# First rows by whole-unit transfers on one queue, and both weight matrices in a four-row interleaved layout, in a fused linear-attention and MLP kernel

## The chip, the cores and the metric

The kernel runs on one core of one Trainium2 chip. The metric is device time in microseconds (us) for one execution, lower is better. Engines are named as in the profile: PE is TensorE (PEld its weight loads, which overlap the matmuls: before, 130.1 us of loads beside 172.8 us of matmuls in a span of 180.5), DVE is VectorE, ACT is ScalarE, POOL is GpSimd and SP is SyncE. A name such as L507 is a line of that kernel's file, so the numbers differ between kernels.

In the lines of the profile, a is alpha and la its logarithm, cum the running sums of la, b and binv their exponentials, qp and kp the scaled q and k, qkT their transposes, at and atm the scores before and after the mask, yps and x the attention's output, xT its transpose, hT the output of layer 1 and acc that of layer 2. An idle matmul works on zeros and is there to keep PE's clock up (46 of them held the granted clock at 1.00 through a wait in which it otherwise fell to 0.50). W_in's 384 rows are three k-tiles of 128.

## The reference

A gated linear attention feeds a two-layer MLP with tanh-GELU. Inputs and output are float32.

```python
# q, k, v, alpha: (4, 8, 768, 48)
for t in range(S):
    state = alpha[:, :, t, :, None] * state + np.einsum('bhd,bhe->bhde', k[:, :, t], v[:, :, t])
    y[:, :, t] = np.einsum('bhd,bhde->bhe', q[:, :, t], state)
x = y.transpose(0, 2, 1, 3).reshape(3072, 384)
h = x @ w_in                                  # w_in  (384, 2048)
g = 0.5 * h * (1.0 + np.tanh(c * (h + 0.044715 * h * h * h)))
out = g @ w_out                               # w_out (2048, 384)
```

## The kernel before

The sequence is cut into chunks of 128 tokens. A chunk of two batch elements is a pair, one batch element of it is a unit; there are 12 pairs. Pairs 0 and 1 are the first chunk, and their attention is the only work that layer 1 (hT = W_in^T x) has to wait for at the start. A scheduler of the kernel's own fixes the order on each engine; the tile framework then adds a semaphore wait wherever an instruction reads what another, or a transfer, wrote.

Rows of pairs 0 and 1 come packed, a transfer for each four heads of a unit, 32 partitions each, on the queues of SP and ACT. W_in and W_out come on GpSimd's queue, in four parts each, and are narrowed to bf16 on the way (a part is 768 KB of float32 in DRAM and 384 KB as it lands).

```python
LOADS = ('gatea0', 'v0', 'gatek0', 'in 0', 'pk1', 'in 1', 'in 2', 'v1', 'in 3', 'out 0', 'out 1', '2a', ...)
RINGS = (('a', 0, 0, 'SP'), ('a', 0, 2, 'ACT'), ('a', 0, 1, 'SP'), ('a', 0, 3, 'ACT'), ...)   # 20 pieces

self.w_in = const.tile([C, self.NKT, self.d_ff], BF16, name="w_in")      # 128 x 3 x 2048
self.w_out = const.tile([C, self.NFT, self.d_model], BF16, name="w_out")  # 128 x 16 x 384

def load_packed(self, n, c, i, j):            # one of four pieces of a pair
    ...
    src = self.src[n][2 * i + j // 2, j % 2 * 4:j % 2 * 4 + 4, c * C:(c + 1) * C]
    {"SP": nc.sync, "ACT": nc.scalar}.get(e, nc.gpsimd).dma_start(
        u[n][32 * j:32 * j + 32].rearrange("g i (o r) d -> g (i o) (r d)", o=2),
        src.rearrange("y (g r) d -> g y (r d)", r=R))

def wait(self, r, m, j):                      # a "gate": GpSimd's queue stops here
    return lambda e: self.nc.gpsimd.tensor_copy(self.gate[:, 0:1], u[r][:, 0, 0, 0:1])

def load_w(self, which, part):
    if which == "in":
        sl = slice(part * w, (part + 1) * w)                              # w = 512 columns
        self.nc.gpsimd.dma_start(
            self.w_in[:, :, sl], self.w_in_dram.rearrange("(j c) n -> c j n", c=self.C)[:, :, sl])
    else:
        self.nc.gpsimd.dma_start(
            self.w_out[:, sl, :], self.w_out_dram.rearrange("(n c) p -> c n p", c=self.C)[:, sl, :])

def layer1(self, f, c, lo, hi, nt):           # one group: six matmuls
    for s in range(2):
        for j in range(self.NKT):
            self.nc.tensor.matmul(h[:, s], self.w_in[:, j, (nt + s) * self.C:(nt + s + 1) * self.C],
                                  self.xT[c][:, j, lo:hi].rearrange("p g t -> p (g t)"), ...)
```

## Time and profile before

| | before |
|---|---|
| median of 3 runs | 181.46 us (180.95 to 181.86) |
| span of the profiled run | 180.5 us, granted PE clock 1.00 |
| PE busy | 172.8 us, 96% of the span |
| first layer-1 matmul | 17.03 us |
| layer 1 of pairs 0 and 1 ends | 33.05 us |
| from there to the end | 147.45 us |

PE is the bound, so a change is read on PE's lane: when does its first real work start, where does it wait, and how long is the part after the start. In the chain of waits, each line is start, duration, and what the end of the kernel hung on then. In the timeline, the bracket tells how long the engine was idle and what ended it.

### The profile page before, as it was taken

Reading aid. Unit: us, or ns where it says so; the run is one execution under the profiler, and the core shown is the slowest. Engines: PE = TensorE matmul, PEld = TensorE weight load, DVE = VectorE, ACT = ScalarE, POOL = GpSimd, SP = SyncE. Lnnn points to the kernel's source line nnn. Section 1 sums busy time; section 2 is a strip of 40 time slices with the busy share of each in tenths; the row PEclk is TensorE's granted clock in tenths of the full one; section 3 lists DMA queues with packets and bytes.
Section 4 is the critical chain, followed back from the end, with each engine's and each line's share of the span. In section 5 each row is a group of like instructions: output and inputs, shape, how many; then the busy total and the mean of one; then the engine's idle time right before and its main releaser. Section 6 shows DMA issues by size and latency. Waiting matters only on the chain.

```text
span 180.5 us, 4489 instructions
## 1 busy us (share of the span) xinstructions
PE 172.8 (96%) x1858; PEld 130.1 (72%) x1861; DVE 96.9 (54%) x201; ACT 129.8 (72%) x214; POOL 61.1 (34%) x68
## 2 busy tenths in 40 slices
PE   7769999999999999999999999999999999999993
PEld 2446769666796787688688779679677687686872
DVE  7476853045769696487499798199255425000000
ACT  3648768974898678848788757887987984491831
POOL 2595847996657766431740500000000000000000
PEclk9999999999999999999999999999999999999999
DMA  5999999999999999999994535543361280311102
GB/s 154 195 246 210 185 236 229 218 217 205 196 317 212 188 265 227 193 243 229 126 235 128 142 99 131 87 120 79 68 155 52 44 205 4 87 44 47 44 0 87
DMA packets 51204, 27.75 MB, mean 154 GB/s; under 512 B 38832, under 2 KB 48240, under 8 KB 51184
## 3 DMA queue, kind: packets, MB, share of 16 engines
q0 software_dynamic: 32096, 17.70, 63.6%
q1 hardware_dynamic: 18512, 9.38, 19.8%
q10 hardware_dynamic: 576, 0.39, 0.7%
q8 instruction: 14, 0.23, 0.6%
q14 instruction: 6, 0.05, 0.1%
HBM read 25.17 MB, written 4.72 MB: 166 GB/s over the span
## 4 chain that ended last, share of the span: by engine, by line
PE 87%; DMA 8%; POOL 2%; ACT 1%; SPq 1%; issue 0%; POOLq 0%
PE hT L508 35%; PE acc L527 34%; DMA w_in<-in_moe_w_in_dram 5%; PE at L426 4%; PE qkT_ps L365 3%; PE yps L483 3%; PE kv L443 2%; PE cum L321 2%; PE yps L480 2%; DMA k<-in_k_dram 2%; DMA a<-in_alpha_dram 1%; PE xT_ps L497 1%; POOL k L248 1%; PE cum L323 1%; SPq L248 1%; PE idle L223 1%
## 5 line engine op out<-in xcount | busy, mean ns | idle before, releaser
L508 PE MATMUL hT<-xT,w_in 128*128 128x256 bf16 x576 | 69.5, 273 | 0.2 <-DMA w_in<-in_moe_w_in_dram 0.2
L527 PE MATMUL acc<-w_out,gT 128*128 128x384 bf16 (+1 forms) x400 | 69.1, 319 | 0.0
L514 ACT ACTIVATE gT<-hT 128x512 bf16<-128x512 f32 x96 | 56.7, 597 | 16.6 <-PE hT L508 13.3
L508 PEld LDWEIGHTS <-w_in 128*128 128x128 bf16 x576 | 54.3, 98 | 7.3 <-DMA w_in<-in_moe_w_in_dram 0.4
L527 PEld LDWEIGHTS <-gT 128*128 128x128 bf16 x400 | 36.6, 97 | 19.3
L433 DVE TENSOR_TENSOR atm<-at,ut 128x512 bf16<-128x512 f32 x48 | 30.0, 683 | 13.5 <-PE at L426 13.5
L355 DVE TENSOR_TENSOR qp<-q,b 128x768 bf16<-128x768 f32 (+1 forms) x15 | 11.9, 796 | 24.6 <-ACT b L344 23.4
L236 POOL DMA_DIRECT2D v<-in_v_dram x13 | 14.6, 1126 | 13.0 <-PE xT_ps L497 7.8
L539 ACT COPY ot<-acc 128x384 f32<-128x384 f32 (+1 forms) x18 | 8.3, 460 | 13.8 <-PE acc L527 12.9
L236 POOL DMA_DIRECT2D q<-in_q_dram x11 | 12.3, 1117 | 12.3 <-DVE xT L501 7.1
L236 POOL DMA_DIRECT2D a<-in_alpha_dram x11 | 12.3, 1118 | 5.2 <-ACT la L304 1.9
L214 ACT ACT_TABLE_LOAD x9 | 11.5, 1283 | 2.8 <-issue 2.6
L344 ACT ACTIVATE b<-cum 128x768 bf16<-128x768 f32 (+1 forms) x15 | 10.3, 684 | 4.5 <-PE cum L323 2.5
L236 POOL DMA_DIRECT2D k<-in_k_dram x11 | 12.3, 1115 | 2.8 <-DMA w_out<-in_moe_w_out_dram 1.1
L355 DVE TENSOR_TENSOR kp<-k,binv 128x768 bf16<-128x768 f32 (+1 forms) x15 | 11.8, 791 | 0.4 <-DMA k<-in_k_dram 0.4
L514 ACT ACT_TABLE_LOAD x9 | 11.5, 1283 | 0.2
L490 ACT CAST x<-yps 128x384 bf16<-128x384 f32 x15 | 7.2, 479 | 5.3 <-PE yps L483 5.2
L344 ACT ACTIVATE binv<-cum 128x768 bf16<-128x768 f32 (+1 forms) x15 | 10.2, 683 | 0.0
L383 DVE COPY qkT<-qkT_ps 128x1024 bf16<-128x1024 bf16 (+1 forms) x12 | 7.9, 687 | 3.9 <-PE qkT_ps L365 3.8
L223 PE MATMUL idle<-zero 128*128 128x512 bf16 x24 | 8.6, 450 | 1.3 <-DVE half L798 1.2
L465 DVE TENSOR_TENSOR stmp<-kv,st 128x384 f32<-128x384 f32 x16 | 8.8, 551 | 1.2 <-PE kv L443 1.2
L468 DVE TENSOR_TENSOR st<-stmp,ends 128x384 bf16<-128x384 f32 x16 | 8.9, 558 | 0.6
(64 smaller groups left out, 161.0 us busy)
## 6 DMA issues: line engine op xcount, KB each, us to landing
out_dram<-ot SPq DMA_DIRECT2D x23, 192.0 KB, 2.3
a<-in_alpha_dram POOLq DMA_DIRECT2D x9, 384.0 KB, 10.9
q<-in_q_dram POOLq DMA_DIRECT2D x9, 384.0 KB, 10.6
k<-in_k_dram POOLq DMA_DIRECT2D x9, 384.0 KB, 11.2
v<-in_v_dram POOLq DMA_DIRECT2D x11, 192.0 KB, 11.2
w_in<-in_moe_w_in_dram POOLq DMA_DIRECT2D x4, 384.0 KB, 8.4
w_out<-in_moe_w_out_dram POOLq DMA_DIRECT2D x4, 384.0 KB, 9.8
a<-in_alpha_dram SPq DMA_DIRECT2D x6, 96.0 KB, 3.7
```

The source lines that it names most:

```text
L214: nc.scalar.add_instruction(mybir.InstLoadActFuncSet(name=nc.get_next_instruction_name(), act_func_set_id=i, engine=mybir.EngineType.Activ ...
L223: self.nc.tensor.matmul(ps, self.zero[:, 0:self.C], self.zero, start=True, stop=True)
L236: (nc.sync if e == "SP" else nc.gpsimd).dma_start(u[n][:, lo:hi].rearrange("t b h d -> t (b h) d"), src)
L344: self.nc.scalar.activation(u[n].rearrange("t i h d -> t i (h d)")[:, lo:hi], cum, AF.Exp, scale=1.0 if n == "b" else -1.0)
L355: self.nc.vector.tensor_tensor(out, rows, b, op=ALU.mult)
L433: self.nc.vector.tensor_tensor(u["atm", i][:, o], u["at", i][o], self.ut[:, None, :].to_broadcast([self.C, self.H // 2, self.C]), op=ALU.mult)
L465: nc.vector.tensor_tensor(s, acc, old, op=ALU.add)
L468: nc.vector.tensor_tensor(new.rearrange("f p (o d) -> f (p o) d", o=2), acc.rearrange("f p (o d) -> f (p o) d", o=2), ends, op=ALU.mult)
L508: self.nc.tensor.matmul(h[:, s], self.w_in[:, j, (nt + s) * self.C:(nt + s + 1) * self.C], self.xT[c][:, j, lo:hi].rearrange("p g t -> p ( ...
L514: return lambda e: self.nc.scalar.activation(self.gT[c % self.NG][:, nt:nt + 2, lo * self.C:hi * self.C], f.pop(("h", c, lo, nt)), AF.Gelu ...
L527: self.nc.tensor.matmul(f["acc", c, b][:, lo:hi], self.gT[c % self.NG][:, nt, b * self.C:(b + 1) * self.C], self.w_out[:, nt, lo:hi], star ...
L539: self.copy(e)(f["ot", c, b][:, sl], f["acc", c, b] if half is None else f["acc", c, b, half][:, sl])
```

## The change

The intent is to start earlier. A unit's rows become one transfer over all 128 partitions on SP's queue, so the first unit can be worked on while the second is in flight; v of pair 0 comes there too, as float32, and is narrowed by an engine; GpSimd is freed for W_in. For this a partition holds four tokens of two heads in another order, and masks and sums are built for it. W_out is put with four neighbouring rows in a partition (source runs of 6 KB instead of 1.5 KB), and since W_out's row order is the order of layer 1's columns, layer 1 must read W_in's columns in steps of four.

```diff
-    LOADS = ('gatea0', 'v0', 'gatek0', 'in 0', 'pk1', 'in 1', 'in 2', 'v1', 'in 3', 'out 0', ...)
-    RINGS = (('a', 0, 0, 'SP'), ('a', 0, 2, 'ACT'), ('a', 0, 1, 'SP'), ('a', 0, 3, 'ACT'), ...)
+    LOADS = ('gatev0', 'in 0', 'in 1', 'v1', 'in 2', 'in 3', 'out 0', ...)
+    RINGS = (('a', 0, 0, 1), ('a', 0, 1, 2), ('q', 0, 0, 1), ('k', 0, 0, 1), ('q', 0, 1, 2), ('k', 0, 1, 2), ('v', 0, 0, 2),
+             ('a', 1, 0, 1), ('a', 1, 1, 2), ('q', 1, 0, 1), ('k', 1, 0, 1), ('q', 1, 1, 2), ('k', 1, 1, 2))
+    NARROW = (0,)
 ...
+            if u["packed"] and n != "v":
+                dma(u[n][:, lo].rearrange("p (o r) d -> p o (r d)", o=2),
+                    src[0, :, c * C:(c + 1) * C].rearrange("h (g r) d -> g h (r d)", r=R))
 ...
-                    self.w_out[:, sl, :], self.w_out_dram.rearrange("(n c) p -> c n p", c=self.C)[:, sl, :])
+                    self.w_out[:, part * w:(part + 1) * w, :], self.w_out_dram.rearrange("(n c r) p -> n c r p", c=self.C, r=w)[part])
 ...
     def layer1(self, f, c, lo, hi, nt):
+            w_in = self.w_in.rearrange("k j (q c r) -> k j q r c", c=self.C, r=self.NFT // 4)
-                    self.nc.tensor.matmul(h[:, s], self.w_in[:, j, (nt + s) * self.C:(nt + s + 1) * self.C],
+                    self.nc.tensor.matmul(h[:, s], w_in[:, j, nt // 4, nt % 4 + s],
 ... (masks, transposes, scheduler costs, and v narrowed on an engine: cut)
```

More of the change, by code (lines that the diff above doesn't have):

```diff
@@ L17 @@
     cum=530, cum_packed=1500, t8=450, t4=225, attn=340, kv=170, inter=170, intra=205, tx=168, l1_4=655, l1_2=340, l2=655,
-    qk2=910, qk1=500, ev8=650, ev4=350, mask=640, st=1090, st0=545, end=110, attn2=590, xc=520, xe=330, ot=540,
+    qk2=910, qk1=500, ev8=650, ev4=350, mask=640, st=1090, st0=545, end=110, attn2=590, vb=320, vb_act=480, ring=1150, ring_v=1900, ring_issue=450, xc=520, xe=330, ot=540,
     ev8_act=960, ev4_act=520, xc_act=450, xe_act=450, ot_act=450,
-    strip=2120, cast=1500, weight=2080, dma=2100, issue=1100, wissue=760, sp=100, store=2600, turn=1250, landed=2200, xbar_qk=1500, xbar_x=1000, late_x=2500, piece=330, late_k=1500, piece_issue=450, begin=2700, cast_0=1300, share=1200, cast_1=1900, ln_packed=1040, cold=380, fill=216, zero=1100,
+    strip=2120, cast=1500, weight=2080, dma=2100, issue=1100, wissue=760, sp=100, store=2600, turn=1250, landed=2200, xbar_qk=1500, xbar_x=1000, late_x=2500, piece=330, late_k=1500, piece_issue=450, begin=3100, cast_0=1300, share=1200, cast_1=1900, ln_packed=1040, cold=380, fill=216, zero=1100,
 )
@@ L143 @@
     EARLY = (0, 1)
-    LOADS = ('gatea0', 'v0', 'gatek0', 'in 0', 'pk1', 'in 1', 'in 2', 'v1', 'in 3', 'out 0', 'out 1', '2a', 'out 2', '2b', 'out 3', '3', '4', '5', '6', '7', '8', '9', '10', '11')
-    PACKED, CUM_FF, R = (0, 1), (1,), 4
-    RINGS = (('a', 0, 0, 'SP'), ('a', 0, 2, 'ACT'), ('a', 0, 1, 'SP'), ('a', 0, 3, 'ACT'), ('q', 0, 0, 'SP'), ('q', 0, 2, 'ACT'), ('q', 0, 1, 'SP'), ('q', 0, 3, 'ACT'), ('k', 0, 0, 'SP'), ('k', 0, 2, 'SP'), ('k', 0, 1, 'SP'), ('k', 0, 3, 'SP'), ('a', 1, 0, 'SP'), ('a', 1, 1, 'SP'), ('a', 1, 2, 'SP'), ('a', 1, 3, 'SP'), ('q', 1, 0, 'SP'), ('q', 1, 1, 'SP'), ('q', 1, 2, 'SP'), ('q', 1, 3, 'SP'))
-    TABLE = ('q', 0, 3)
+    LOADS = ('gatev0', 'in 0', 'in 1', 'v1', 'in 2', 'in 3', 'out 0', 'out 1', '2a', 'out 2', '2b', 'out 3', '3', '4', '5', '6', '7', '8', '9', '10', '11')
+    PACKED, CUM_FF, R = (0, 1), (0, 1), 4
+    RINGS = (('a', 0, 0, 1), ('a', 0, 1, 2), ('q', 0, 0, 1), ('k', 0, 0, 1), ('q', 0, 1, 2), ('k', 0, 1, 2), ('v', 0, 0, 2),
+             ('a', 1, 0, 1), ('a', 1, 1, 2), ('q', 1, 0, 1), ('k', 1, 0, 1), ('q', 1, 1, 2), ('k', 1, 1, 2))
+    NARROW = (0,)
     TURN_QK, TURN_X = (8, 9, 10, 11), (7, 8, 9, 10, 11)
@@ L157 @@
     BUFS = dict(ca=1, yk=2, ff=4, la=3, qp=4, kp=4, b8=2, kn=2, qkT=4, atm=6, x=3, ot=6, bend=3, ends=8,
-                a=4, q=4, k=4, v=6)
+                a=4, q=4, k=4, v=1, vb=6)
     def __init__(self, ctx, tc, q, k, v, alpha, w_in, w_out, out):
@@ L227, in load @@
     def load(self, n, c, i, lo=0, hi=2):
-        nc, C, H, D = self.nc, self.C, self.H, self.D
-        u = self.p[c, i]
-        def emit(e):
-            if n not in u:
-                u[n] = self.tile(n, [C, 2, H, D], BF16 if n == "v" else F32)
-            src = self.src[n][2 * i + lo:2 * i + hi].rearrange("b h s d -> s (b h) d")[c * C:(c + 1) * C]
-            (nc.sync if e == "SP" else nc.gpsimd).dma_start(u[n][:, lo:hi].rearrange("t b h d -> t (b h) d"), src)
-        return emit
-    def load_packed(self, n, c, i, j):
         nc, C, H, D, R = self.nc, self.C, self.H, self.D, self.R
@@ L244, in emit @@
         def emit(e):
-            if n not in u:
-                u[n] = self.tile(n, [C, 2, H, D], F32)
-            src = self.src[n][2 * i + j // 2, j % 2 * 4:j % 2 * 4 + 4, c * C:(c + 1) * C]
-            {"SP": nc.sync, "ACT": nc.scalar}.get(e, nc.gpsimd).dma_start(
-                u[n][32 * j:32 * j + 32].rearrange("g i (o r) d -> g (i o) (r d)", o=2),
-                src.rearrange("y (g r) d -> g y (r d)", r=R))
+            t = "vb" if n == "v" and u["m"] not in self.NARROW else n
+            if t not in u:
+                u[t] = self.tile(t, [C, 2, H, D], BF16 if t == "vb" else F32)
+            dma = (nc.sync if e == "SP" else nc.gpsimd).dma_start
+            src = self.src[n][2 * i + lo:2 * i + hi]
+            if u["packed"] and n != "v":
+                dma(u[n][:, lo].rearrange("p (o r) d -> p o (r d)", o=2),
+                    src[0, :, c * C:(c + 1) * C].rearrange("h (g r) d -> g h (r d)", r=R))
+            else:
+                dma(u[t][:, lo:hi].rearrange("t b h d -> t (b h) d"), src.rearrange("b h s d -> s (b h) d")[c * C:(c + 1) * C])
         return emit
@@ L266, in emit @@
                 w = self.NFT // 4
-                sl = slice(part * w, (part + 1) * w)
                 self.nc.gpsimd.dma_start(
-                    self.w_out[:, sl, :], self.w_out_dram.rearrange("(n c) p -> c n p", c=self.C)[:, sl, :])
+                    self.w_out[:, part * w:(part + 1) * w, :], self.w_out_dram.rearrange("(n c r) p -> n c r p", c=self.C, r=w)[part])
         return emit
@@ L326, in cum, with narrow, emit @@
         return emit
+    def narrow(self, u, lo, hi):
+        def emit(e):
+            if "vb" not in u:
+                u["vb"] = self.tile("vb", [self.C, 2, self.H, self.D], BF16)
+            self.copy(e)(u["vb"][:, lo:hi].rearrange("t b h d -> t (b h d)"), u["v"][:, lo:hi].rearrange("t b h d -> t (b h d)"))
+        return emit
     def exp(self, u, n, lo, hi):
@@ L335, in emit @@
                 out = u[n][:, lo:hi]
-                if u["packed"]:
-                    out = u[n].rearrange("f i (w z) -> f z (i w)", z=2)[:, lo]
+                out = out[:, 0] if u["packed"] else out
                 self.nc.scalar.activation(out, u["cum"][lo][:, H * D:H * D + H // 2] if u["packed"] else
@@ L380, in emit @@
             if u["packed"]:
-                t = self.qkT(u)[:, "qk".index(which)].rearrange("f i (w z) (g r) -> f z (i w) g r", z=2, r=self.R)[:, i]
-                ps = ps[:, 0].rearrange("f r (w g) -> f w g r", g=32)
+                t = t[:, 0].rearrange("f j (g r) -> f j g r", r=self.R)
+                ps = ps[:, 0].rearrange("f r (g j) -> f j g r", j=4)
             self.copy(e)(t, ps)
@@ L443, in emit @@
                 nc.tensor.matmul(kv[:, p, :], u["kn" if u["packed"] else "kp"][:, i, 2 * p:2 * p + 2, :].rearrange("t h d -> t (h d)"),
-                                 u["v"][:, i, 2 * p:2 * p + 2, :].rearrange("t h d -> t (h d)"),
+                                 u["vb"][:, i, 2 * p:2 * p + 2, :].rearrange("t h d -> t (h d)"),
                                  start=True, stop=True)
@@ L482, in emit @@
             for h in range(H):
-                nc.tensor.matmul(y[:, h, :], u["atm", i][:, h % 2, h // 2, :], u["v"][:, i, h, :],
+                nc.tensor.matmul(y[:, h, :], u["atm", i][:, h % 2, h // 2, :], u["vb"][:, i, h, :],
                                  start=c == 0, stop=True, skip_group_check=True)
@@ L559, in load @@
             nonlocal n
-            land = W[{"v": "cast", "w": "weight"}.get(key[0], "strip")]
-            loads[key] = s.add("load", {"POOL": cost}, n, emit, gate, land=W[f"cast_{key[1]}"] if key[0] == "v" and key[1] in self.PACKED else land * 3 // 8 if key[0] != "w" and key[1] in self.SPLIT else land,
-                               late=W["share"] if key[:2] == ("v", 0) else 0)
+            land = W["weight" if key[0] == "w" else "cast" if key[0] == "v" else "strip"]
+            loads[key] = s.add("load", {"POOL": cost}, n, emit, gate, land=W["cast_1"] if key[0] == "v" and key[1] in self.PACKED else land * 3 // 8 if key[0] != "w" and key[1] in self.SPLIT else land)
             n += 1
@@ L575, in weights @@
                 load(("w", which, part), W["wissue"], self.load_w(which, part))
-        for r, m, j, e in self.RINGS:
-            loads[r, m, j] = s.add("load", {e: W["piece_issue"]}, n, self.load_packed(r, *pairs[m], j), land=W["piece"] + (0 if n else W["begin"]))
+        for m, x in enumerate(pairs):
+            self.p[x].update(m=m, packed=m in self.PACKED)
+        s.add("table", {"ACT": W["table"]}, n, lambda e: self.act_set(LN_EXP))
+        for r, m, lo, hi in self.RINGS:
+            loads[r, m, lo] = loads[r, m, hi - 1] = s.add(
+                "load", {"SP": W["ring_issue"]}, n, self.load(r, *pairs[m], lo, hi), land=(W["ring_v" if r == "v" else "ring"] * (hi - lo) // 2 if n else W["begin"]))
             n += 1
-            if (r, m, j) == self.TABLE:
-                s.add("table", {"ACT": W["table"]}, n, lambda e: self.act_set(LN_EXP))
         for step in self.LOADS:
@@ L584, in tasks @@
                 rows(int(step[1:]), "v")
-            elif step[0] == "p":
-                r, m = step[1], int(step[2])
-                for j in range(4):
-                    loads[r, m, j] = s.add("load", {"POOL": W["piece_issue"]}, n, self.load_packed(r, *pairs[m], j), gate, land=W["piece"] + (0 if j else W["late_k"]))
-                    n += 1
             elif step[:4] == "gate":
-                key = step[4], int(step[5]), int(step[6:] or 3)
+                key = step[4], int(step[5]), 1
                 gate = [s.add("gate", {"POOL": 150}, n, self.wait(*key), [loads[key]])]
@@ L599, in tasks @@
                 weights(*step.split())
-        def rows_of(r, m, j):
-            return [loads[r, m, w] for w in range(4)] if m in self.PACKED else [loads[r, m, j]]
         states, ys, xts, lns, ends, ats = {}, {}, {}, {}, {}, {}
@@ L607, in tasks @@
             u, P = self.p[c, i], 100 * m
-            u["m"] = m
-            u["sums"], u["packed"], u["apart"] = c < NCH - 1, m in self.PACKED, m in self.CUM_FF
+            u["sums"], u["apart"] = c < NCH - 1, m in self.CUM_FF
             early = m in self.EARLY
@@ L614, in tasks @@
                 n = hi - lo
-                ln = s.add("ln", {"ACT": W["ln_packed" if u["packed"] else "ln"] * n // 2}, P, self.ln(u, lo, hi), rows_of("a", m, lo), LN_EXP)
+                ln = s.add("ln", {"ACT": W["ln_packed" if u["packed"] else "ln"] * n // 2}, P, self.ln(u, lo, hi), [loads["a", m, lo]], LN_EXP)
                 cum = s.add("cum", {"PE": W["cum_packed" if u["packed"] else "cum"] * n // 2}, P - 400, self.cum(u, lo, hi), [ln])
@@ L626, in tasks @@
                 for j in range(lo, hi, step):
-                    qp[j:j + step] = [s.add("qp", {"DVE": W[f"qk{step}"]}, P + 5 + 5 * j, self.scaled(u, "q", j, j + step),
-                                            [x[0], *rows_of("q", m, j)])] * step
+                    qp[j:j + step] = [s.add("qp", {"DVE": W[f"qk{step}"]}, P + (5 + 4 * j if u["packed"] else 5 + 5 * j), self.scaled(u, "q", j, j + step),
+                                            [x[0], loads["q", m, j]])] * step
                 for j in range(lo, hi, step):
-                    kp[j:j + step] = [s.add("kp", {"DVE": W[f"qk{step}"]}, P + 6 + j, self.scaled(u, "k", j, j + step),
-                                            [x[1], *rows_of("k", m, j)])] * step
+                    kp[j:j + step] = [s.add("kp", {"DVE": W[f"qk{step}"]}, P + (6 + 4 * j if u["packed"] else 6 + j), self.scaled(u, "k", j, j + step),
+                                            [x[1], loads["k", m, j]])] * step
             for r, users in (("a", lns[m]), ("q", qp), ("k", kp)):
@@ L642, in tasks @@
             exps[0].take("b8", *qp, *kp)
+            if m == 1:
+                cums[1].deps.append(ys[1, 0])
             vs, kvs, tq, cs, users, turns, masks = [], [], [], [], [], [], {}
@@ L646, in tasks @@
                 owner, turned = tq[0], tq
-            if u["packed"]:
-                every, backs = [], []
-                for n, d in (("q", qp), ("k", kp)):
-                    for j in range(2):
-                        t1 = s.add("t", {"PE": W["t4"]}, P + 10, self.turn(u, j, n), [d[j]])
-                        every.append(s.add("ev", {"DVE": W["ev4"] + 270, "ACT": W["ev4_act"] + 80}, P + 10, self.turned(u, j, n), [t1]))
-                        t1.take("yk", every[-1])
-                        tq.append(t1)
-                owner = every[0]
+            backs = []
+            vin = [loads["v", m, j] for j in range(2)]
+            if m in self.NARROW:
+                vin = [s.add("vb", {"DVE": W["vb"], "ACT": W["vb_act"]}, P + 19, self.narrow(u, j, j + 1), vin[j:j + 1]) for j in range(2)]
             if u["sums"]:
@@ L659, in tasks @@
                 o, k = P + 10 + 3 * j, kp[j]
-                if u["packed"]:
-                    turned = every
-                elif m not in self.TURN_QK:
+                if m not in self.TURN_QK:
                     turned = []
+                    o -= 3 * u["packed"]
                     for which in ("q", "k") if early else ("qk",):
                         n = 4 * len(which)
-                        cost = {"DVE": W[f"ev{n}"]}
+                        cost = {"DVE": W[f"ev{n}"] + 270 * u["packed"]}
                         if m in self.EV_ACT:
-                            cost["ACT"] = W[f"ev{n}_act"]
+                            cost["ACT"] = W[f"ev{n}_act"] + 80 * u["packed"]
                         t1 = s.add("t", {"PE": W[f"t{n}"]}, o, self.turn(u, j, which),
@@ L691, in tasks @@
                 y = s.add("y", {"PE": W["intra"] + (W["inter"] if c else 0)}, P + 20 + j, self.y(u, j, c, b),
-                          ms + turned + [loads["v", m, j]] + ([states[b, c - 1]] if c else []))
+                          ms + turned + [vin[j]] + ([states[b, c - 1]] if c else []))
                 xc = s.add("x", {"ACT": W["xc_act"], "DVE": W["xc"]}, P + 20 + j, self.x(u, j), [y])
@@ L712, in tasks @@
                         backs.append(tb)
-                    kv = s.add("kv", {"PE": W["kv"]}, P + 30 + j, self.kv(u, j), [k, loads["v", m, j]])
+                    kv = s.add("kv", {"PE": W["kv"]}, P + 30 + j, self.kv(u, j), [k, vin[j]])
                     st = states[b, c] = s.add("st", {"DVE": W["st" if c else "st0"]}, P + 30 + j, self.carry(u, j, c, b),
@@ L730, in tasks @@
             kp[0].take("kp", *tq, *kvs)
-            loads["v", m, 0].take("v", *vs)
+            if m in self.NARROW:
+                loads["v", m, 0].take("v", *vin)
+                vin[0].take("vb", *vs)
+            else:
+                loads["v", m, 0].take("vb", *vs)
             if u["sums"]:
@@ L791, in run @@
     def run(self):
-        nc = self.nc
+        nc, C = self.nc, self.C
         self.tasks()
@@ L800, in run @@
             nc.vector.memset(self.half[64 * o:64 * o + 64, o:o + 1], 1.0)
-        nc.vector.memset(self.blk, 0.0)
-        for t in self.ut_blk:
-            nc.vector.memset(t, 0.0)
-        for p in range(4):
-            nc.vector.memset(self.blk[32 * p:32 * p + 32, p:p + 1], 1.0)
-        for p in range(4):
-            a, b = 32 * p, 32 * p + 32
-            nc.vector.tensor_copy(self.ut_blk[1][a:b, a:b], self.ut_h[a:b, a:b])
-            nc.vector.tensor_copy(self.ut_blk[0][a:b, a + 1:b], self.ut_h[a:b, a:b - 1])
+        nc.vector.tensor_reduce(self.blk, self.ident.rearrange("p (g j) -> p j g", j=4), axis=mybir.AxisListType.X, op=ALU.max)
+        same = self.blk[:, None, :].to_broadcast([C, C // 4, 4])
+        nc.vector.tensor_tensor(self.ut_blk[1].rearrange("p (g j) -> p g j", j=4), self.ut_h.rearrange("p (g j) -> p g j", j=4), same, op=ALU.mult)
+        nc.vector.tensor_tensor(self.ut_blk[0], self.ut_blk[1], self.ident, op=ALU.subtract)
         for i in range(max(self.BUFS[n] for n in self.ring)):
```

## The prediction

> **What bounds the kernel now.** I read the strip of 40 slices first (4.5 us a slice; digits are tenths busy).
>
> ```profile
> PE   7769999999999999999999999999999999999993
> ...
> DMA  5999999999999999999994535543361280311102
> ```
>
> TensorE (PE) is full from the fourth slice to the end; only the first three have holes, and some of what fills those is the "idle" matmul that only keeps the clock up. The table of stretches agrees: from 60 to 120 us PE is busy 60.00 of 60.00 us, from 36 to 60 us 23.71 of 24.00. The instruction order shows that after about 30 us both kernels have the same work in the same order on every engine. So the change can win only what it takes from the start, unless it changes a duration of the steady part. I then read the chain of waits in order of time (start, us, what):
>
> ```profile
> 4.58 3.13 DMA k<-in_k_dram
> ...
> 8.43 0.68 POOL w_in L263
> 9.11 2.21 POOL k L248 x4
> 11.32 8.31 DMA w_in<-in_moe_w_in_dram
> 19.68 0.83 PE hT L508 x6
> ```
>
> GpSimd waits for pair 0's k, issues the first W_in part, spends 2.21 us issuing pair 1's k, and only then asks for the second W_in part, which PE meets at 19.68. Last, the timeline of the start, where the attention of pairs 0 and 1 is made:
>
> ```profile
> 4.08 0.94 ACT L302 ACTIVATE la<-a 128x384 f16<-128x384 f32 x2 [0.15 <-DMA a<-in_alpha_dram]
> ...
> 6.34 0.49 ACT L344 ACTIVATE b<-cum 128x384 bf16<-128x384 f32 x1 [1.33 <-PE cum L293]
> ...
> 7.83 1.03 DVE L355 TENSOR_TENSOR kp<-k,binv 128x384 bf16<-128x384 f32 x2 [0.40 <-DMA k<-in_k_dram]
> ...
> 10.99 2.48 DVE L433 TENSOR_TENSOR atm<-at,ut 128x512 bf16<-128x512 f32 x4 [0.77 <-PE at L426]
> ...
> 12.06 0.94 ACT L302 ACTIVATE la<-a 128x384 f16<-128x384 f32 x2 [1.51 <-DMA a<-in_alpha_dram]
> ...
> 14.16 0.36 PE L483 MATMUL yps<-v,atm 128*128 128x48 bf16 x8
> ...
> 17.03 0.82 PE L508 MATMUL hT<-xT,w_in 128*128 128x256 bf16 x6
> ```
>
> A four-head packing makes each row tensor of a pair four transfers of 32 partitions, and nothing starts before all four are there (4.08). The exponential waits 1.33 us because both units' sums lie in one PSUM tile. The masks end at 13.47, but yps comes at 14.16, behind the sums of pair 1, which waited for their rows until 12.06. The first layer-1 matmul runs at 17.03, the sixteenth group of them ends at 33.05, and from there PE is full.
>
> [...] The trace of before has weight loads of 98 ns, packed ones only; none shows the step. [...] In the trace SyncE's pieces of 32 partitions ran at 202 to 224 GB/s at 5 to 7 us, and at 229 to 280 when ScalarE's queue carried other partitions beside them; but each 98 KB issue takes 0.43 us, which alone caps one queue at 229 GB/s[...]
>
> **Part by part.**
> *Rows.* Partition is now 4 x group + head pair, so one unit (one batch element) is one transfer of 196 KB over 128 partitions. Twelve such and v0 on SyncE replace 16 SyncE, 4 ScalarE, 4 GpSimd pieces and a v. Before, the first two pieces (together 196 KB) landed 2.52 us after 0.74, at 3.26. I take the same for a of unit 0, then 0.6 us a transfer[...]: a1 3.9, q0 4.5, k0 5.1, q1 5.7, k1 6.3. For v0 with its 192-byte rows I take the 226 GB/s of the row stage from 36 to 60 us: 393 KB, 1.75 us, about 8.0. Pair 1 then lands between 8.7 and about 14, its tail sharing with W_in. Its k was used first at 17.84 before.
> *Pair 0.* ln at 3.3 instead of 4.08 (-0.8), unit by unit; sums 3.85 to 4.9; b at 4.95 instead of 6.34 (-1.4), as each unit's sums have their own tile. DVE from there, with the old durations in the new order: qp 5.5, kp 6.0, copy of k^T 7.05 to 7.75, qp and kp of unit 1 to 8.8, ends, mask, copy, three masks (0.62 us apart, 0.69 the copy): 12.1 instead of 13.47. So half the head start is kept; DVE is the limit, as unit 0's transposed copy now costs it an idle 0.5. v0's two narrowing copies (0.48 us each, like the x copy) go on ScalarE at 8.0 and 9.4, where it has room. After the masks: xT copy 12.9, x 13.35, qp of pair 1 13.9, second xT 14.3: first hT at about 14.65 instead of 17.03 (-2.4). The wait of yps for pair 1's rows is gone.
> *W_in.* GpSimd's gate moves from k0 (7.86) to v0 (about 8.1), so the first part is issued near 8.2, before 8.37: no gain. But the second follows at 9.0, not 11.3, since the k pieces are gone. At 20 to 24 us the cast queue alone wrote 200 GB/s, so 2.0 us a part of 393 KB. With first data at 9.9 and 3 to 4 us beside pair 1's rows: parts at 13.5, 15.6, (v1 17.2), 19.2, 21.2. My walk through the new PE order needs them at 14.65, 16.6, 20.3, 22.1. They just come in time, with about 1 us to spare.
> *Pair 1.* Between 17.03 and 33.05 PE took 16.0 us for 16 groups of 0.656 us (10.5) and the attention's pieces (k^T, kv, at, yps, xT: 3.8): 14.3 of work and 1.7 of waits and idle fills. The walk through the new order, with the old durations (hT groups 0.66, transposes 0.22 for four, at 0.33, yps 0.3, DVE's copy 0.69, mask 0.62, state 0.55): groups 1 and 2 to 15.95; transposes and an idle piece; group 3 at 16.6 to 17.3; at of unit 0 at 17.3, behind DVE's copy of k^T (16.45 to 17.15, after qp, kp and kn); group 4 at 18.05; at of unit 1 at 18.9, behind ScalarE's last copy, which waits for the table load (15.15 to 16.4) and three gelus (to 18.2). DVE does the four masks with two state updates between them from 17.85 to 21.5. PE meanwhile: yps at 19.8, groups 5 and 6 from 20.3, yps of unit 1 at 21.8, group 7 at 22.1, its transposes at 22.85, group 8 from 23.0, k back 0.45. So xT of pair 1 is copied at 23.5 (26.77 before), and the ninth group begins at 24.1, not 27.3 (-3.2). Layer 1 of both pairs then ends at about 29.8, not 33.05: **-3.2 us**. PE's floor from 14.65 (14.5 us of work) would be 29.15, a gain of 3.9.
> *W_out.* Four neighbouring rows per partition make source runs of 6 KB out of 1.5 KB. [...] w_out was never waited for: first use 33.05, and in the new run near 29.8 with landing near 23 to 24 (estimate at 2 us a part behind W_in). Worth 0 by itself[...].
> *Setup.* Fifteen small DVE operations become three, off the path.
> *After 33 us.* Same order, 147.45 us of it to the end: 0. Sum: -3.2; I take 0.2 off for semaphore hops that a hand walk misses: **-3.0, 178.4 us (-1.7%)**.
>
> **Rivals.**
> 1. *The strided weight read is slow.*
>
> ```profile
> L508 PE MATMUL hT<-xT,w_in 128*128 128x256 bf16 x576 | 69.5, 273 | 0.2 <-DMA w_in<-in_moe_w_in_dram 0.2
> ...
> L508 PEld LDWEIGHTS <-w_in 128*128 128x128 bf16 x576 | 54.3, 98 | 7.3 <-DMA w_in<-in_moe_w_in_dram 0.4
> ```
>
> Six matmuls take 0.656 us, a pitch of 109 ns, so the 98 ns load hides with 11 ns to spare. Each ns over that costs 576 ns in all; a load of 130 ns would cost 12 us and lose everything. [...] 5%.
> 2. *DMA becomes the bound.* It is full from 2 us on, and the bytes before the ninth group are the same. [...] rows and W_in come 2 to 3 us later, and PE waits for W_in: gain about 1, 180.5 us. Also the rows of pairs 2 and 3 are wanted 3 us earlier: la of pair 3 ran at 41.14, its rows issued at 31.44 with 9 to 11 us to land, little slack. 20%.
> 3. *DVE's and ScalarE's in-order queues stall*, a narrowing copy before la or an at before a mask: each 0.5 us, gain 2 to 2.5. 25%.
> 4. *Better than thought:* pair 1 never blocks PE, gain 3.7 to 4: 177.6. 25%.
>
> **Range and chances.** Over 2% is a gain above 3.63 us, under 177.83: rival 4 and a part of the centre, 0.32. A loss above 3.6 us needs rival 1: 0.05. The rest 0.63. Eight in ten between 176.6 and 180.2.
>
> **What would show it.** First ln near 3.3, b near 5.0; v0 landed near 8; masks of pair 0 ended near 12; first hT near 14.65; ninth group near 24; end of the 96 hT near 29.8; then the same 147.4 us. Wrong if LDWEIGHTS of w_in is above 109 ns or the hT group above 0.66 us; if PE waits over 0.5 us for W_in or w_out; or if the stretch after layer 1 of pair 1 isn't 147.4 us long.

## The result

| | before | after |
|---|---|---|
| median, 4 runs each | 181.66 us (180.95 to 181.86) | 192.20 us (190.92 to 192.73) |
| span of the profiled run | 180.5 | 190.2 |
| mean granted PE clock | 1.00 | 0.964 (0.972 in one run) |
| layer 1 of pairs 0 and 1 ends | 33.05 | 42.71 |
| from there to the end | 147.45 | 147.49 |

The changed kernel is slower: the ratio is 1.058 (95% interval 1.052 to 1.064). A ratio here is always the mean time of one kernel's runs over that of the other's of the same rounds, so not quite the ratio of the medians quoted. Executions over 1.5% slower than the fastest of the same kernel are left out of the means.

The strip of 40 slices of the changed kernel, 4.75 us a slice, with the granted clock in tenths:

```profile
PE   6991079999999999999999999999999999999993
...
PEclk9997558999999999999999999999999999999999
DMA  4999999999999999897299362726146144210102
```

PE has a hole in the fourth to sixth slice, about 14 to 28 us, where there was none. The clock falls to half in it: 0.61 from 16 to 18 us, 0.50 from 18 to 26. DMA is full all the while (9 tenths or more in each of these slices).

The chain of waits of the changed kernel in order of time:

```profile
4.16 0.61 SPq L240
4.82 4.82 DMA v<-in_v_dram
9.69 0.18 POOL gate L249
9.87 1.58 POOL w_in L256 x2
11.45 1.17 POOL vb L243
12.62 0.72 POOL w_in L256
13.35 11.72 DMA w_in<-in_moe_w_in_dram
25.20 2.51 PE hT L507 x11
27.71 0.85 PE qkT_ps L363 x8
...
38.78 3.93 PE hT L507 x36
42.71 2.60 PE acc L526 x16
```

GpSimd issues parts 0 and 1 of W_in, v of pair 1, and parts 2 and 3; then the whole kernel waits 11.72 us for the **last** of these transfers. Before, the same chain went through the second part at 19.68. The timeline of the start, changed kernel:

```profile
3.76 0.52 ACT L294 ACTIVATE la<-a 128x384 f16<-128x384 f32 x1 [1.74 <-DMA a<-in_alpha_dram]
...
5.90 0.49 ACT L342 ACTIVATE b<-cum 128x384 bf16<-128x384 f32 x1 [0.85 <-PE cum L285]
...
9.66 0.51 ACT L324 CAST vb<-v 128x384 bf16<-128x384 f32 x1 [1.14 <-DMA v<-in_v_dram]
...
13.96 0.36 DVE L499 COPY xT<-xT_ps 128x384 bf16<-128x384 bf16 x1
...
17.86 0.40 PE L507 MATMUL hT<-xT,w_in 128*128 128x256 bf16 x1 [3.10 <-DMA w_in<-in_moe_w_in_dram]
...
19.02 0.56 DVE L353 TENSOR_TENSOR kp<-k,binv 128x384 bf16<-128x384 f32 x1 [3.33 <-DMA k<-in_k_dram]
...
25.20 2.51 PE L507 MATMUL hT<-xT,w_in 128*128 128x256 bf16 x11 [6.95 <-DMA w_in<-in_moe_w_in_dram]
```

The attention of pair 0 really is earlier: its second xT copy ends at 14.32, against 16.76 before. But one hT matmul runs at 17.86 when the first W_in part is there, and the **next** one, which reads the same 512 columns, waits until 25.20. The eleven matmuls there take 2.51 us, 228 ns each, twice the usual pitch (start of one to start of the next) of 109 ns. Busy time by stretch, changed kernel (stretch, length, then PE, PEld, DVE, ACT, POOL busy with counts, granted clock, DMA share, GB/s), and after it the long stretch:

```profile
16.00:18.00 2.00, 0.14 (x1) 0.11 (x1) 0.00 (x0) 0.37 (x1) 0.16 (x1) 0.61 1.42 194
18.00:20.00 2.00, 0.26 (x1) 0.00 (x0) 0.65 (x2) 0.00 (x0) 0.90 (x1) 0.50 1.92 178
...
42.71:190.20 147.49, 144.33 (x1555) 115.05 (x1553) 77.46 (x137) 107.97 (x171) 31.08 (x28) 1.00 0.68 128
```

The same stretch of the kernel before:

```profile
33.05:180.50 147.45, 144.18 (x1555) 109.71 (x1553) 77.42 (x137) 107.98 (x171) 39.79 (x35) 1.00 0.76 142
```

The two long stretches have the same 1555 matmuls and the same length to 0.04 us, though PEld is 5.3 us busier in the changed one. So the whole difference, 42.71 - 33.05 = 9.66 us, lies ahead of the end of layer 1. The groups on the page of the changed kernel (busy us, mean ns, idle before and what ended it) name it:

```profile
L507 PE MATMUL hT<-xT,w_in 128*128 128x256 bf16 x576 | 71.7, 277 | 10.0 <-DMA w_in<-in_moe_w_in_dram 10.0
...
L507 PEld LDWEIGHTS <-w_in 128*128 128x128 bf16 x576 | 61.4, 114 | 12.7 <-issue 7.5
```

hT now waits 10.0 us for W_in (0.2 before), and the stepped weight load costs 114 ns instead of 98. Which of the two cost the time is not told by the sum of either. The list of instructions of the two built programs, which has no times but names every semaphore that a PE instruction waits for, does tell. Its weight loads of W_in that wait for a GpSimd transfer (row, line, wait; DMASWn is a semaphore of GpSimd's transfers, which a later transfer uses again, as DMASW1 for the first and the fourth part before):

```
before   257 L508 Ldweights w_in [waits DMASW1_49]
         313 L508 Ldweights w_in [waits DMASW6_49]
         369 L508 Ldweights w_in [waits DMASW7_49]
         455 L508 Ldweights w_in [waits DMASW1_49]
after    245 L507 Ldweights w_in [waits DMASW0_49]
         247 L507 Ldweights w_in [waits DMASW4_49,DMASW3_49,DMASW1_49]
```

Before, four waits stand apart, one for each part. After, the second weight load of all waits for the other three parts at once. It reads `w_in[:, 1, 0, 0]`, the first 512 columns of the second k-tile, and needs none of them. The theory is a false wait: the framework seems to take the stepped read of k-tile 1 or 2 to touch what the other transfers write. The rivals are the stepped weight load itself, the half clock, and the rows' transfers crowding W_in.

### The profile page after: what moved, and what is told of

It is laid out like the page before. It is cut to its first block, busy times and chain, and to the rows that moved or that the text cites. A ratio compares the mean times of both kernels' runs of the same rounds, so it can differ in the third digit from the quotient of the medians.

```text
span 190.2 us, 4443 instructions
## 1 busy us (share of the span) xinstructions
PE 174.8 (92%) x1851; PEld 137.5 (72%) x1854; DVE 97.2 (51%) x191; ACT 130.0 (68%) x214; POOL 56.3 (30%) x62
## 4 chain that ended last, share of the span: by engine, by line
PE 85%; DMA 9%; SPq 2%; POOL 2%; ACT 1%; issue 0%
PE hT L507 34%; PE acc L526 33%; DMA w_in<-in_moe_w_in_dram 6%; PE qkT_ps L363 3%; PE at L424 3%; DMA v<-in_v_dram 3%; PE yps L481 2%; PE kv L441 2%; SPq L240 2%; PE cum L313 2%; PE yps L478 2%; POOL w_in L256 1%; PE xT_ps L495 1%; PE cum L315 1%; POOL vb L243 1%; PE idle L224 1%
## 5 line engine op out<-in xcount | busy, mean ns | idle before, releaser
L507 PE MATMUL hT<-xT,w_in 128*128 128x256 bf16 x576 | 71.7, 277 | 10.0 <-DMA w_in<-in_moe_w_in_dram 10.0
L507 PEld LDWEIGHTS <-w_in 128*128 128x128 bf16 x576 | 61.4, 114 | 12.7 <-issue 7.5
L526 PEld LDWEIGHTS <-gT 128*128 128x128 bf16 x400 | 36.7, 97 | 19.2
L353 DVE TENSOR_TENSOR qp<-q,b 128x768 bf16<-128x768 f32 (+1 forms) x15 | 11.9, 795 | 23.9 <-ACT b L342 21.0
L243 POOL DMA_DIRECT2D vb<-in_v_dram x12 | 13.3, 1109 | 18.3 <-PE xT_ps L495 15.2
L381 DVE COPY qkT<-qkT_ps 128x1024 bf16<-128x1024 bf16 (+1 forms) x13 | 8.5, 686 | 11.3 <-PE qkT_ps L363 11.2
L353 DVE TENSOR_TENSOR kp<-k,binv 128x768 bf16<-128x768 f32 (+1 forms) x15 | 11.9, 791 | 3.3 <-DMA k<-in_k_dram 3.3
L488 ACT CAST x<-yps 128x384 bf16<-128x384 f32 x13 | 6.2, 476 | 4.4 <-PE yps L481 4.4
L488 DVE CAST x<-yps 128x384 bf16<-128x384 f32 x11 | 6.1, 556 | 5.8 <-PE yps L481 5.7
## 6 DMA issues: line engine op xcount, KB each, us to landing
w_out<-in_moe_w_out_dram POOLq DMA_DIRECT2D x4, 384.0 KB, 11.4
```

What stands on the lines that cost most here:

```text
L243: dma(u[t][:, lo:hi].rearrange("t b h d -> t (b h) d"), src.rearrange("b h s d -> s (b h) d")[c * C:(c + 1) * C])
L353: self.nc.vector.tensor_tensor(out, rows, b, op=ALU.mult)
L381: self.copy(e)(t, ps)
L488: self.copy(e)(x, u["y", i].rearrange("t h d -> t (h d)"))
L507: self.nc.tensor.matmul(h[:, s], w_in[:, j, nt // 4, nt % 4 + s], self.xT[c][:, j, lo:hi].rearrange("p g t -> p (g t)"), start=j == 0, sto ...
L526: self.nc.tensor.matmul(f["acc", c, b][:, lo:hi], self.gT[c % self.NG][:, nt, b * self.C:(b + 1) * self.C], self.w_out[:, nt, lo:hi], star ...
```

## The experiments

All eleven kernels gave the right output. They ran in three batches, each compared with runs of the kernel before on the same chip: medians 181.89 (part outermost, rows alone, weights alone, 46 idle matmuls), 181.50 (eight idle matmuls, the gates on q and a of pair 0, steps of eight) and 181.70 us (part outermost on the old rows, the two later gates; seven of these eight runs are those of the second batch). The first batch had another chip than the other two.

### The weights' tile with the part outermost

The changed kernel, with W_in's tile laid out so that each part is a slice of its own; the step of four stays.

```diff
-        self.w_in = const.tile([C, self.NKT, self.d_ff], BF16, name="w_in")
+        self.w_in = const.tile([C, 4, self.NKT, self.d_ff // 4], BF16, name="w_in")
-                    self.w_in[:, :, sl], self.w_in_dram...
+                    self.w_in[:, part], self.w_in_dram...
-            w_in = self.w_in.rearrange("k j (q c r) -> k j q r c", c=self.C, r=self.NFT // 4)
+            w_in = self.w_in[:, nt // 4].rearrange("k j (c r) -> k j r c", c=self.C)
-                    ... w_in[:, j, nt // 4, nt % 4 + s],
+                    ... w_in[:, j, nt % 4 + s],
```

> The changed kernel with W_in held in SBUF part by part (part outermost, then k-tile, then 512 columns) and nothing else changed: the same transfers, the same steps of four in the weight loads. Theory A (a false wait: the stepped read of W_in makes the second weight load wait for all four W_in transfers): the wait of 6.9 us at 25.2 is gone, groups of layer 1 run as the parts land (17.8, 20.1, 23.4, 25.1), layer 1 of both pairs ends near 33.5, time 181 to 183.5. Rival B (the stepped weight load itself is slow, 113 instead of 98 ns): stays at 188 or more. Rival C (the W_in parts come late because of the rows): as A, but not under 182.

Measured: 181.44, 182.66 us in two fast runs and 184.67, 185.59 in two slow ones at a clock of 0.98; ratio 1.010 (1.003 to 1.017). The built program waits for the four parts apart again (rows 245, 287, 395, 441). Its chain:

```profile
10.33 8.46 DMA w_in<-in_moe_w_in_dram
18.84 0.84 PE hT L507 x6
...
28.20 3.93 PE hT L507 x36
32.13 2.60 PE acc L526 x16
```

The chain goes through the second part again, at 18.84, and layer 1 ends at 32.13 instead of 42.71: 10.6 us come back in the profiled runs through a change of addresses alone. This run is the fastest of the four, and its W_in parts also landed 1.0 to 1.6 us earlier than the changed kernel's, which a later kernel with the same tile does not repeat (17.7 for the first part, below). The ratio to the kernel before falls from 1.058 to 1.010, which is 8.6 us. The weight load still has 114 ns and 36 matmuls still take 3.93 us. So the loss was the false wait, not the stepped load. But of the predicted 3.2 us against before (33.05) only 0.9 appears in this run, and over the runs nothing.

### The rows alone

The changed kernel with before's W_out order and contiguous W_in reads.

```diff
-... self.w_out_dram.rearrange("(n c r) p -> n c r p", c=self.C, r=w)[part])
+... self.w_out_dram.rearrange("(n c) p -> c n p", c=self.C)[:, part * w:(part + 1) * w, :])
-                    ... w_in[:, j, nt // 4, nt % 4 + s],
+                    ... self.w_in[:, j, (nt + s) * self.C:(nt + s + 1) * self.C],
```

> The changed kernel with the weights as before: W_out rows 128 apart, W_in columns read in a row; only the rows' transfers are new. Theory A: no false wait, 181 to 183.5, within 1 us of the kernel with W_in part by part; weight loads 98 ns. Rival C (the rows on SyncE's queue hold up the weights): 184 or more.

Measured: 182.75 us (181.92 to 183.18), ratio 1.005 (1.002 to 1.008). Weight load 98 ns; layer 1 ends at 33.65. Its chain:

```profile
9.48 7.21 DMA w_in<-in_moe_w_in_dram
16.73 2.45 PE hT L506 x12
```

The new row transfers, without any false wait, bring nothing and are if anything 0.5% slower: pair 0's attention is ready early, and PE then idles for 1.9 us until the first part lands at 16.73. The first twelve hT took 2.45 us there, where the first experiment's fast run had 1.50: the clock had dropped in the wait (8 and 7 tenths in the two slices of its strip from 13.6 to 22.6 us, 9 in every slice of the other's).

### The weights alone

The kernel before, with the new W_out order and the stepped reads of W_in in one tile.

```diff
-... self.w_out_dram.rearrange("(n c) p -> c n p", c=self.C)[:, sl, :])
+... self.w_out_dram.rearrange("(n c r) p -> n c r p", c=self.C, r=w)[part])
+            w_in = self.w_in.rearrange("k j (q c r) -> k j q r c", c=self.C, r=self.NFT // 4)
-                    ... self.w_in[:, j, (nt + s) * self.C:(nt + s + 1) * self.C],
+                    ... w_in[:, j, nt // 4, nt % 4 + s],
```

> The kernel before with the new weights only (W_out four rows per partition, W_in in steps of four), its rows untouched. Theory A: the second weight load of layer 1 waits for the last W_in part, near 24.9; from there as in the changed kernel (17.5 us to the end of layer 1 of both pairs, at half clock first): ends near 42, time 189 to 192. If the rows are the cause: 181 to 182.

Measured: 190.78 us (190.60 to 191.55), ratio 1.050 (1.048 to 1.053). Its chain:

```profile
15.66 8.03 DMA w_in<-in_moe_w_in_dram
23.73 1.25 PE hT L509 x5
```

With the old row transfers the same stop appears: one hT at 16.74, the other five of its group at 23.73. The loss comes in with the weights' layout and needs nothing of the new rows.

### The weights' layout with the part outermost, on the old rows

The previous kernel with the tile of the first experiment (the same edit), five rounds.

> The kernel before with the new weights (four W_out rows per partition, W_in in steps of four) and W_in held part by part, its rows as before: what the layout of the weights is worth without the false wait. Theory A: no wait for all parts, so the 8.9 us that the weights alone cost (190.8) are gone; W_out's longer runs are off the path: 181 to 182, same as before within 0.5%. If W_out's runs of 6 KB free DMA time that the start needs: under 180.5.

Measured: 181.93 us (181.19 to 182.58), ratio 1.001 (0.997 to 1.006); layer 1 ends at 32.58. The 8.9 us of the previous experiment are gone. The groups on its page:

```profile
L509 PE MATMUL hT<-xT,w_in 128*128 128x256 bf16 x576 | 69.6, 273 | 0.0
...
L509 PEld LDWEIGHTS <-w_in 128*128 128x128 bf16 x576 | 60.8, 113 | 1.2
```

All 576 loads are stepped, 113 ns each, and the matmuls of hT are as busy as before (69.5 us there), with no wait for W_in. The W_out order with its stepped reads is worth nothing and costs nothing that these runs can tell (W_out's transfers took 9.3 us from issue to landing in the median, 9.8 before, one run each, and no matmul waited for them).

### Steps of eight

The changed kernel with eight W_out rows per partition and W_in read in steps of eight, in one tile. The longer step is to show whether the load grows with it, and the built program waits differently: row 245 for parts 0 and 1, row 395 for parts 2 and 3, which here is right, since a read in steps of eight spans two parts.

```diff
-... self.w_out_dram.rearrange("(n c r) p -> n c r p", c=self.C, r=w)[part])
+... self.w_out_dram.rearrange("(n c r) p -> n c r p", c=self.C, r=2 * w)[part // 2][:, part % 2 * w:(part % 2 + 1) * w])
-            w_in = self.w_in.rearrange("k j (q c r) -> k j q r c", c=self.C, r=self.NFT // 4)
+            w_in = self.w_in.rearrange("k j (q c r) -> k j q r c", c=self.C, r=self.NFT // 2)
-                    ... w_in[:, j, nt // 4, nt % 4 + s],
+                    ... w_in[:, j, nt // 8, nt % 8 + s],
```

> The changed kernel with eight neighbouring W_out rows per partition and W_in columns read in steps of eight, so 16 bytes apart: measures the stepped weight load by itself. The step of four took 113 ns against 98 for neighbouring columns, hidden under a pitch of 109 ns. If the load grows with the step, 130 ns or more, and six hT matmuls then take more than 0.656 us (0.78 at 130 ns), the stretch after layer 1 of pair 1 grows from 147.5 us by 576 times the excess. If the step does not matter further: 113 ns and the time of the changed kernel, 191 to 193.

Measured: 187.39 us, one run, its state unknown. The weight load took 144 ns in the median. The timeline:

```profile
20.22 2.75 PE L507 MATMUL hT<-xT,w_in 128*128 128x256 bf16 x12 [5.90 <-DMA w_in<-in_moe_w_in_dram]
```

PE starts when the second part is there, as its list of waits says, and layer 1 ends at 37.53, about midway between 32.13 and 42.71. So the time follows the list of waits in both directions.

```profile
33.58 3.95 PE hT L507 x36
37.53 2.60 PE acc L526 x16
```

And 36 hT matmuls take 3.95 us, 109.7 ns each, under loads of 144 ns: the loads are nearly hidden although each lasts longer than the pitch. What they cost is at most the 0.6 us by which the stretch after layer 1 is longer (148.07 us against 147.49, one run each), where 576 times the excess of 35 ns over the pitch would be 20 us. A build in steps of two, not run, has the same false wait as steps of four.

### Keeping the clock up

The changed kernel with 46 idle matmuls ahead of the first layer-1 group; then the first experiment's kernel with eight of them.

```diff
+            if (c, lo, nt) == (0, 0, 0):
+                self.fill(46)("PE")        # 8 in the second kernel
```

> The changed kernel with 46 idle matmuls ahead of the first group of layer 1, so that TensorE's clock stays up during the wait. Theory A says the wait for the last W_in part stays (25.2); the clock is 1.0 from there, and the pieces from 25.2 to 30 run at full speed: 2.3 us less (hT x11 1.2 instead of 2.51, transposes 0.45 instead of 0.85, hT x6 0.66 instead of 1.26), time 189.5 to 190.5. If the clock is the main cause and not the wait: under 186.

Measured: 191.25 us (190.49 to 192.03), ratio 1.052 (1.049 to 1.056), clock 0.998 to 1.00. Its chain:

```profile
25.79 1.36 PE hT L509 x11
...
40.93 2.60 PE acc L528 x16
```

The eleven hT matmuls after the wait took 1.36 us instead of 2.51, and layer 1 ended at 40.93 instead of 42.71. From the end of the wait to the end of layer 1 it is 15.14 us instead of 17.51. So the half clock is a result of the wait (with the idle matmuls in it the granted clock was 1.00 from 16 to 30 us) and 2.4 us of its cost in that stretch; the last part landed 0.6 us later here, which leaves 1.8. Most of these 1.8 us do not reach the end: the rest of the profiled run was 149.4 us instead of 147.5, with two waits, 2.0 us together, for a transposing transfer (qkT from kp) that is not in the changed kernel's chain. I have not explained them.

> The kernel with W_in part by part, plus 8 idle matmuls (1.7 us) ahead of the first group of layer 1. In e1 the runs spread from 181.4 at clock 1.0 to 185.6 at 0.981, and TensorE stood idle from 14.7 to 16.3. If that spread is the clock dropping in the wait for the first W_in part, the idle work keeps it at 1.0 in every run: 181 to 182, spread under 1 us. If the spread has another cause (transfers): it stays.

Measured: 182.86 us (182.30 to 184.01), ratio 1.008 (1.002 to 1.013), clock 0.999 to 1.00 in every run. The slow runs of the first experiment, at 0.98, are gone, so those most likely came from its idle 1.6 us before layer 1 and the clock after it (none of them was profiled, and the two kernels ran on different chips). The median is not under before's even so. In the profiled run, the slowest, the clock was full, the first W_in part landed only at 17.7 and layer 1 ended at 34.72: in this run at least, what is left is the transfers.

### When W_in may start

The first experiment's kernel with GpSimd's gate on other rows, to see whether the fourth W_in part can come sooner.

```diff
-    LOADS = ('gatev0', ...
+    LOADS = ('gateq0', ...    # or 'gatea0', 'gatea1' (waiting for unit 1), 'gatek1'
```

> The kernel with W_in part by part, with GpSimd's gate on pair 0's q (landed near 6.9) and not on v0 (9.3): W_in is asked for 2.4 us earlier. If the time of asking set its arrival: first part near 14, first group of layer 1 near 14.6, end of layer 1 of both pairs near 30.5, 180 to 181. If the DMA engines' rate sets it (same bytes to move before it): parts 3 and 4 come as before, v0 and pair 1's rows later, 181.5 to 183.

> As the run with the gate on q, but on the second unit's alpha (landed near 4.5): 5 us earlier than on v0. By the first theory the first part near 12 and 179.5 to 180.5, unless v0 then lands after 11 and holds yps back; by the rate theory 181.5 to 184.

> The kernel with W_in part by part, with GpSimd's gate on pair 1's alpha, second unit (landing near 10.7), 1.4 us later than v0. The runs with an earlier gate showed W_in on GpSimd's queue holding up the rows on SyncE's (v0 at 14.3 and 17.3 instead of 9.3). If so, a later gate brings pair 1's q and k earlier (k of unit 1 before 16 instead of 17.5) and the W_in parts no more than 1 us later: 181 to 182.5. If bytes alone set the arrival: fourth part near 24 as before.

> As the run with the gate on pair 1's alpha, on pair 1's k (near 12.5): the rows are nearly through before W_in starts. First W_in part near 17, and layer 1 starts with it: 182 to 184. If sharing the engines wasted time, the parts follow 2.0 us apart and the fourth comes before 24.5.

| gate on | gate at | v of pair 0 | W_in part 0 | W_in part 3 | layer 1 ends | median us | ratio |
|---|---|---|---|---|---|---|---|
| a of pair 0 | 3.78 | 17.33 | 11.4 | 24.7 | 44.19 | 193.49 | 1.067 |
| q of pair 0 | 5.33 | 14.29 | 13.6 | 25.3 | 36.24 | 185.13 | 1.019 |
| v of pair 0 (first experiment) | 9.28 | 9.24 | 16.3 | 24.2 | 32.13 | 183.66 | 1.010 |
| a of pair 1, unit 1 | 10.78 | 9.66 | 18.2 | 25.9 | 36.16 | 185.15 | 1.019 |
| k of pair 1 | 11.92 | 9.29 | 17.3 | 24.8 | 32.72 | 183.53 | 1.010 |

(us; landings are read from the timeline as the start of what waited for them. The gates on a and q of pair 0 and on k of pair 1 read unit 0's rows, so they opened at the earlier of the two. The profiled run of the gates on v and on k of pair 1 is the fastest of its kernel; the median of the gate on v is over two runs counted as slow too, and its ratio is not. So compare the columns of landings with each other, and medians with medians.) The timeline of the kernel gated on a of pair 0:

```profile
17.33 0.51 ACT L324 CAST vb<-v 128x384 bf16<-128x384 f32 x1 [9.44 <-DMA v<-in_v_dram]
...
24.42 1.47 PE L507 MATMUL hT<-xT,w_in 128*128 128x256 bf16 x12
```

Two things follow. An early gate does bring the first W_in part forward, to 11.4, but it pushes v of pair 0 back by 8 us, from 9.24 to 17.33, and with it all of pair 0; the chain of that run then waits for q of pair 1, until 30.16. The gate on a of pair 1 loses otherwise: PE is idle for 3.33 us ahead of the first part, and the first groups run at half clock (0.50 from 18 to 22 us).

```profile
18.19 2.75 PE hT L507 x12
```

And the fourth part lands between 24.2 and 25.9 whether the gate opens at 3.8 or at 11.9; before it was 24.9. DMA is full in all these runs and moved 189 to 201 GB/s over their first 24 us. No gate tried was better than the change's own by more than its spread. That the fourth part is held by the byte rate of the DMA engines is my reading of this table and not shown: I did not change the number of bytes. One of the runs speaks against its simplest form: with the gate on a of pair 0, a k and a q of pair 1 landed only at 26.95 and 30.19, behind the fourth part, so fewer rows were ahead of it, and it still came no sooner than 24.7.

## Why the prediction was wrong

| step | before | predicted | after |
|---|---|---|---|
| first ln | 4.08 | 3.3 | 3.76 |
| b of unit 0 | 6.34 | 4.95 | 5.90 |
| v of pair 0 landed | about 13.15 | 8.0 | 9.66 |
| pair 0's masks end | 13.47 | 12.1 | 12.42 |
| pair 0's last xT copied | 16.76 | 14.3 | 14.32 |
| W_in parts landed | 16.2, 19.7, 21.7, 24.9 | 13.5, 15.6, 19.2, 21.2 | 17.9, 20.2, 23.5, 25.2 |
| first hT | 17.03 | 14.65 | 17.86 |
| ninth group of hT | 27.47 | 24.1 | 37.13 |
| 16 groups of hT end | 33.05 | 29.8 | 42.71 |
| from there to the end | 147.45 | 147.4 | 147.49 |

**Pair 0 was right.** Its single steps were up to 1.7 us late (an issue on SP took 0.61 us, not the 0.43 of the half-size pieces, and the first sums ran for 1.44 us where the second took 1.05), but the end of the chain at 14.3 was met. That is in part luck: b came 0.95 us late and the masks ended 0.3 late, and the steps behind them ran that much faster than worked out. The 0.6 us that I gave each transfer of rows was an estimate and not shown by the trace of before: here the second alpha landed at 4.52, 0.76 us after the first. **The stretch after layer 1 was right.**

**The step that failed is "They just come in time, with about 1 us to spare."** It compared each W_in part's landing with the moment when its own group needs it. That took for granted that the changed reads still wait part by part. The diff shows the same bytes read by the same group, so this looked safe; the list of waits shows that the second read waits for all four. That list was there to be read before predicting; I had used it for the order alone. The false wait cost 8.9 us of the median on the old rows (190.78 against 181.89 in the same rounds) and 8.6 by the ratios on the new ones (first experiment; 10.6 of layer 1's end in the two profiled runs).

**The same step was mis-sized without the false wait too.** I gave the parts 13.5 to 21.2 us. With the waits mended (the fast run of the first experiment) they landed at 16.3, 18.8, 22.3 and 24.2, so PE was idle for 1.6 us before its first hT, and layer 1 ended at 32.13, not 29.8. About 1.3 us of the first part's delay is the gate (issue at 9.51 instead of 8.2, since v of pair 0 was late). I take the rest for sharing, which no run isolates: 6 us from the end of the issue at 10.33 to the landing at 16.3, where I gave 4.5. I had written that DMA is full from 2 us on and that "the bytes before the ninth group are the same", as rival 2, and drew only a 20% chance from it. Its figures, W_in 2 to 3 us later and a gain of about 1, are those of the first experiment's profiled run. It should have been the main line: in the runs with five gates, issuing sooner on a full DMA moved the order of landings, hardly the last of them (24.2 to 25.9).

**Rival 1 named the right sign for a wrong reason.** "Each ns over that costs 576 ns in all" is refuted: loads of 113 ns left the pitch at 109 ns (3.93 us for 36), and loads of 144 ns left it at 109.7. So "A loss above 3.6 us needs rival 1: 0.05" was wrong in its logic and not only in its size. No trace had shown a stepped load, so its chance of 5% was my own estimate. The test "if PE waits over 0.5 us for W_in" did fire, at 10.0 us. So did "above 109 ns" for the weight load, at 113, but by itself that meant nothing: at full clock the hT group stayed at 0.66 us. Rivals 3 and 4 were not what happened, and no matmul waited for W_out (acc idled 0.0 us), as predicted.

**What stays open:** why the tracking takes a step of four or two to touch all parts and a step of eight not (only its result was seen), and the 2.0 us of waits of the kernel with 46 idle matmuls. No version tried beats the kernel before; the mended layout on the old rows equals it.

## What to carry to other kernels

After a change of a tile's view, compare the list of semaphore waits of the two builds, not only the order of instructions: a stepped view across a tile that several transfers fill can wait for all of them, and giving each transfer an outermost slice of its own mended it here at no cost (ratio 1.001 on the old rows). Where DMA is already full, ask whether the last transfer that is needed will land sooner at all; here issuing it earlier gained nothing (the last part landed between 24.2 and 25.9 with the gate anywhere from 3.78 to 11.92). That fewer bytes would have gained was not tested. A weight load of 113 or 144 ns (98 packed) hardly showed in the time, since the pitch of its matmuls stayed near 109 ns (109.7 with the longer one), so read the pitch before blaming the load.
